# Moving GpSimd's copies, the DMA transposes and ScalarE's joins of k and q within a RetNet and SiLU-MLP kernel

## The chip, the cores and the metric

The kernel runs on one core of a Trainium2 chip. The metric is the device time of one execution in microseconds (us), the median over executions. Spans in traces are some 1.8 us shorter than these times.

## The reference, cut to what matters

```python
# q, k, v: (4, 8, 768, 64) float32; w_in: (512, 2048); w_out: (2048, 512)
for t in range(S):                                  # recurrence, one decay gamma per head
    state = gamma * state + k[:, :, t] (outer) v[:, :, t]
    y[:, :, t] = scale * q[:, :, t] @ state
x = y.transpose(0, 2, 1, 3).reshape(B * S, H * D)   # 3072 x 512
h = x @ w_in
out = (h * sigmoid(h)) @ w_out
```

## The kernel before

The recurrence is done in chunks of 128 steps. A *unit* is one chunk of one batch, 24 in all. Unit m is worked on in *visits*: visit m prepares it, visit m+1 forms its scores, visit m+2 its outputs `y`. Visits stand between *products*: a product is 12 matmuls of 128x512 for one block of the first MLP layer, 2.72 us on TensorE. In the later part there are four products from one visit to the next.

From unit 17 on, k and q are transposed by the DMA, not by TensorE. That takes three steps per tensor: GpSimd parts the float32 words into 16-bit planes, a DMA transposes the planes, ScalarE joins them again. In the code below `n` counts the products, and `far[n]` is the unit whose visit stands behind product n. (TensorE's order is the program's; a list scheduler orders the other engines' queues, within the given limits.)

```python
def fence(done, then):                # one group of y matmuls must wait for another
    i = nc.gpsimd.memset(token, 0.0).ins
    tc.add_manual_dep(i, done.name, sync, reason="fence")
    tc.add_manual_dep(then, i.name, sync, reason="fence")

def part_t(n):                        # GpSimd: q, then k
    ... nc.gpsimd.tensor_copy(out=planes, in_=words)
def turn_t(n):                        # DMA, from the sync queue: q, then k
    ... nc.sync.dma_start_transpose(out=turned, in_=planes)
def join_t(name, n):                  # ScalarE
    ... nc.scalar.copy(out=words, in_=turned)

def product_in(c, f):
    ha, hb = turn(...), turn(...)     # 2 of 3 PSUM banks, in rotation
    ... 8 matmuls into ha, 4 into hb
    hs = hpool.tile(...)              # 3 buffers
    copied[:] = [nc.scalar.activation(out=hs, in_=ha, ...)]      # "evacuation"
    ... behind_copy: the joins
    taken_out[:] = [nc.vector.tensor_tensor(out=hs, in0=hs, in1=hb, op=ALU.subtract)]
    ... behind_next: scaling of k, weight conversion
    nc.scalar.activation(out=hs, in_=hs, func=AF.Silu)

def next_chunk():                     # once in four units: gq, the decay of q, for the next chunk
    for a in range(HP):
        nc.scalar.activation(out=gq[:, a, :], in_=gq[:, a, :], func=AF.Copy, scale=step[:, a:a+1])

for n, (c, f) in enumerate(steps):
    if n - 2 in far:
        behind_copy.append(lambda m=far[n - 2]: join_t("q", m))
        behind_next.append(lambda m=far[n - 2]: scale_k(m))
    if n - 3 in far:
        behind_copy.append(lambda m=far[n - 3]: join_t("k", m))
    product_in(c, f)
    ...
    put_g(1)                          # sync queue: store the product before this one
    behind.get((c, f), lambda: None)()          # the visit, if one stands here
    if n in far:
        turn_t(far[n])
    if n + 1 in far:
        part_t(far[n + 1])
```

## Time and profile before

| | kernel before |
|---|---|
| time, median of 3 runs | 635.18 us (634.76 to 635.78) |
| TensorE busy | 604.1 of 632.9 us |
| TensorE's waits on the fence's memset | 6.0 us |
| GpSimd copies | 14, of 1.03 to 1.91 us |

GpSimd's `token` memsets, one per visit, are marks in time. I call the stretch from the memset of visit 15 (187.72 us in this trace) to that of visit 25 (316.02 us) the *region*: the changed code lies within it, ten stages of 128.30 us together. From the last memset to the end another 316.88 us pass.

The memset distances, in us (stage 16 is the one that ends with the memset of visit 16):

| stage | 16 | 17 | 18 | 19 | 20 | 21 | 22 | 23 | 24 | 25 | sum |
|---|---|---|---|---|---|---|---|---|---|---|---|
| before | 9.95 | 8.73 | 14.43 | 13.87 | 13.87 | 14.15 | 13.84 | 13.51 | 13.19 | 12.76 | 128.30 |

### The profile page before, as it was taken

What the parts mean: (1) busy time and instruction counts of PE and PEld (TensorE: products, weight loads), DVE (VectorE), ACT (ScalarE), POOL (GpSimd) and SP (SyncE); (2) the same over time, 40 slices, a digit from 0 to 9 for tenths busy, and PEclk for the clock granted to TensorE, in tenths of its full rate; (3) what the DMA queues carried; (4) which work ended last, traced back from release to release, by engine and by line L of the source; (5) the groups of instructions that cost most, each with busy time, mean ns of one, the idle gap of its engine ahead of it and who ended that gap; (6) DMA issues with size and microseconds to landing.
All of it is one profiled execution on the core that took longest, in us unless ns stands there. A gap on an engine that the chain in (4) does not pass through costs nothing.

```text
span 632.9 us, 13500 instructions
## 1 busy us (share of the span) xinstructions
PE 604.1 (95%) x5384; PEld 498.5 (79%) x5384; DVE 427.2 (68%) x732; ACT 311.3 (49%) x583; POOL 25.5 (4%) x79
## 2 busy tenths in 40 slices
PE   5788999999999899999999999999999999999997
PEld 3667888887887777778788888888888888888785
DVE  2897997798978868788778674463635544554631
ACT  6657896676565556566568761321312221412311
POOL 3000000000002201121000000000000000000000
PEclk9998999999999999999999999999999999999999
DMA  9996896455678889999757643342433423342301
GB/s 201 212 216 162 233 241 212 160 163 186 221 192 201 219 240 230 235 269 273 248 183 230 189 138 129 111 156 67 165 102 102 166 79 121 134 133 89 111 1 66
DMA packets 137998, 107.31 MB, mean 170 GB/s; under 512 B 94800, under 2 KB 103248, under 8 KB 137936
## 3 DMA queue, kind: packets, MB, share of 16 engines
q1 hardware_dynamic: 135056, 101.21, 56.7%
q10 hardware_dynamic: 2880, 5.24, 2.2%
q8 instruction: 42, 0.69, 0.5%
q14 instruction: 20, 0.16, 0.1%
HBM read 66.06 MB, written 36.70 MB: 162 GB/s over the span
## 4 chain that ended last, share of the span: by engine, by line
PE 86%; DVE 5%; issue 3%; DMA 2%; SPq 1%; ACT 1%; POOL 0%; ACTq 0%; DVEq 0%; POOLq 0%
PE ha L580 25%; PE o L738 20%; PE oa L738 14%; PE hb L580 12%; PE ob L738 7%; PE y L456 4%; PE sc L413 2%; PE sc L423 1%; SPq L149 1%; DMA wf<-in_moe_w_in_dram 1%; DMA kqv<-in_q_dram 1%; PE qp L397 1%; DVE g L588 1%; PE kp L397 1%; DMA wf<-in_moe_w_out_dram 0%
## 5 line engine op out<-in xcount | busy, mean ns | idle before, releaser
L580 PE MATMUL ha<-xt,wi 128*128 128x512 f32 x768 | 193.5, 394 | 0.0
L580 PEld LDWEIGHTS ha<-xt,wi 128*128 128x128 f32 x768 | 143.5, 189 | 31.1 <-DVE g L588 0.5
L738 PE MATMUL o<-wo,gs 128*128 128x512 f32 x576 | 146.3, 389 | 0.0
L738 PEld LDWEIGHTS o<-wo,gs 128*128 128x128 f32 x576 | 108.1, 188 | 22.4
L637 DVE TENSOR_TENSOR gs<-gr,gs 128x512 fp32r<-128x512 f32 x96 | 62.2, 686 | 90.8 <-ACT gs L635 90.8
L635 ACT ACTIVATE gs<-gr 128x512 fp32r<-128x512 f32 x96 | 53.4, 621 | 134.8 <-issue 132.4
L738 PE MATMUL oa<-wo,gs 128*128 128x512 f32 x384 | 118.3, 389 | 0.0
L580 PE MATMUL hb<-xt,wi 128*128 128x512 f32 x384 | 102.9, 390 | 0.5 <-ACT g L584 0.5
L588 DVE TENSOR_TENSOR g<-g,hb 128x512 f32<-128x512 f32 x96 | 65.7, 684 | 40.8 <-ACT g L584 22.7
L580 PEld LDWEIGHTS hb<-xt,wi 128*128 128x128 f32 x384 | 72.0, 188 | 16.0 <-ACT g L584 0.9
L738 PEld LDWEIGHTS oa<-wo,gs 128*128 128x128 f32 x384 | 72.1, 188 | 15.0
L592 ACT ACTIVATE g<-g 128x512 f32<-128x512 f32 x96 | 60.6, 631 | 39.4 <-DVE g L588 39.3
L738 PE MATMUL ob<-wo,gs 128*128 128x512 f32 x192 | 75.2, 392 | 0.4 <-DVE o L747 0.4
L584 ACT ACTIVATE g<-ha 128x512 f32<-128x512 f32 x96 | 56.9, 592 | 32.0 <-PE ha L580 20.9
L638 DVE SCALAR_TENSOR_TENSOR gs<-gs 128x512 fp32r<-128x512 f32 x96 | 62.0, 685 | 0.0
L738 PEld LDWEIGHTS ob<-wo,gs 128*128 128x128 f32 x192 | 36.0, 188 | 9.4 <-DVE o L747 2.1
L197 ACT ACTIVATE ca<-wf 128x512 f32<-128x512 f32 x32 | 21.6, 674 | 15.1 <-DMA wf<-in_moe_w_out_dram 5.6
L456 PE MATMUL y<-qt,state 64*64 64x64 f32 x320 | 17.7, 226 | 7.8 <-POOL token L339 6.0
L456 PE MATMUL y<-qt,mid 64*64 64x64 f32 x384 | 21.8, 227 | 1.6 <-issue 1.6
L208 DVE SCALAR_TENSOR_TENSOR cp<-wf,cp 128x512 f32<-128x512 uint32 x32 | 22.7, 710 | 0.6
L204 DVE SCALAR_TENSOR_TENSOR cs<-ca,cs 128x512 uint32<-128x512 uint32 x32 | 22.1, 691 | 0.9
L746 ACT ACTIVATE o<-o 128x512 f32<-128x512 f32 x10 | 6.0, 600 | 33.4 <-PE o L738 33.0
(84 smaller groups left out, 555.5 us busy)
## 6 DMA issues: line engine op xcount, KB each, us to landing
gd<-g SPq DMA_DIRECT2D x96, 256.0 KB, 3.1
gr<-gd SPq DMA_DIRECT2D x96, 256.0 KB, 2.7
wf<-in_moe_w_out_dram SPq DMA_DIRECT2D x16, 512.0 KB, 4.8
out_dram<-o ACTq DMA_DIRECT2D x20, 256.0 KB, 2.1
wf<-in_moe_w_in_dram SPq DMA_DIRECT2D x16, 256.0 KB, 3.9
wf<-in_moe_w_in_dram SPq DMA_DIRECT2D x32, 128.0 KB, 4.2
kf<-in_k_dram SPq DMA_DIRECT2D x16, 256.0 KB, 4.5
qf<-in_q_dram SPq DMA_DIRECT2D x16, 256.0 KB, 3.9
```

Source lines behind the costliest of these rows:

```text
L197: nc.scalar.activation(out=a.bitcast(FP32), in_=hi.bitcast(FP32), func=AF.Abs, scale=65536.0)
L204: nc.vector.scalar_tensor_tensor(out=s, in0=a, scalar=3, in1=s, op0=ALU.logical_shift_left, op1=ALU.bitwise_or)
L208: nc.vector.scalar_tensor_tensor(out=p.bitcast(FP32), in0=lo, scalar=2.0 ** -52, in1=p.bitcast(FP32), op0=ALU.mult, op1=ALU.mult)
L456: i = nc.tensor.matmul(yp[ts(e, D), o, a, :], lhsT=lhsT, rhs=rhs, start=(e, o) not in started, stop=True, skip_group_check=True).ins
L580: nc.tensor.matmul(hb if i == 2 else ha, lhsT=w_sb[f][:, i, ts(kk, 128)], rhs=xt[c][:, i, kk, :], start=kk == 0 and i != 1, stop=kk == KIN ...
L584: copied[:] = [nc.scalar.activation(out=hs, in_=ha, func=AF.Copy, scale=ONE_E).ins]
L588: taken_out[:] = [nc.vector.tensor_tensor(out=hs, in0=hs, in1=hb, op=ALU.subtract).ins]
L592: nc.scalar.activation(out=hs, in_=hs, func=AF.Silu)
L635: nc.scalar.activation(out=t[:, 0, :], in_=g, func=AF.Copy, scale=HALF)
L637: nc.vector.tensor_tensor(out=t[:, 1, :], in0=g, in1=high, op=ALU.subtract)
L638: nc.vector.scalar_tensor_tensor(out=t[:, 2, :], in0=t[:, 1, :].bitcast(FP32), scalar=-1.0 / EPS, in1=high, op0=ALU.mult, op1=ALU.add)
L738: nc.tensor.matmul(o, lhsT=g, rhs=wo[f][:, i, :], start=first_ and i != 1, stop=last and i != 0)
```

## The change

Its intent: take GpSimd's copies out of the path from the fence's memset to TensorE. A unit's copies now come behind the memset of its own visit, the transposes one product behind the visit, and both joins behind the third product's evacuation.

```diff
@@ fence
         i = nc.gpsimd.memset(token, 0.0).ins
+        fenced[:] = [i]
@@ visit
             finish_y(m - 2, yp)
+
+        if FAR <= m < len(units):
+            with tc.issue_after(fenced[0]):
+                part_t(m)
@@ the loop over products
         if n - 2 in far:
-            behind_copy.append(lambda m=far[n - 2]: join_t("q", m))
             behind_next.append(lambda m=far[n - 2]: scale_k(m))
         if n - 3 in far:
-            behind_copy.append(lambda m=far[n - 3]: join_t("k", m))
+            behind_copy.append(lambda m=far[n - 3]: [join_t(name, m) for name in "qk"])
...
-        if n in far:
-            turn_t(far[n])
-        if n + 1 in far:
-            part_t(far[n + 1])
+        if n - 1 in far:
+            turn_t(far[n - 1])
```

More of the change, by code (lines that the diff above doesn't have):

```diff
@@ L317 @@
     behind_next, behind_copy, half_split = [], [], []
-    taken_out, copied, masked = [], [], []
+    taken_out, copied, masked, fenced = [], [], [], []
     state, steps_of = {}, {}
```

## The prediction

> **What bounds the kernel now.** I read the page first (engine shares and slices), then the waits of TensorE, then GpSimd's timeline, then the chain of waits around a few visits, and last the busy times by stage.
>
> The page's first lines say that TensorE is nearly everything:
>
> ```profile
> span 632.9 us, 13500 instructions
> ...
> PE 604.1 (95%) x5384; PEld 498.5 (79%) x5384; DVE 427.2 (68%) x732; ACT 311.3 (49%) x583; POOL 25.5 (4%) x79
> ```
>
> TensorE is idle for 632.9 - 604.1 = 28.8 us. No change that leaves its matmuls alone, as this one does, can win more than that, and over a third of the 28.8 us lies in the first 55 us, before the changed code begins. What TensorE waited for:
>
> ```profile
> PE y L456 <- issue: 7.7, 7, 1.8
> PE kp L397 <- DMA kqv<-in_k_dram: 7.5, 4, 4.1
> PE y L456 <- POOL token L339: 6.0, 9, 1.1
> ```
>
> (Columns: us in total, times, longest.) The "issue" and k-load rows are all before 54 us. The third row is this change's: a "visit" interleaves the recurrence of one unit (a 128-step chunk of one batch) between the 2.72 us products of the first matmul layer. In it a group of `y` matmuls must wait for another, and the fence between them goes through GpSimd: a one-element memset on `token` that waits for a matmul and releases one. Of its nine waits, seven lie between 194 and 291 us. GpSimd's timeline shows what precedes them (columns: start, duration, engine, line, operation, tiles, count, idle before and its releaser):
>
> ```profile
> 187.72 0.09 POOL L339 MEMSET token<- 1x1 f32 x1 [8.59 <-PE y L456]
> 196.17 1.56 POOL L373 COPY qp<-qf 128x1024 uint16<-128x1024 uint16 x1 [8.36 <-ACT g L592]
> 197.67 0.09 POOL L339 MEMSET token<- 1x1 f32 x1
> ...
> 233.72 1.04 POOL L373 COPY qp<-qf 128x1024 uint16<-128x1024 uint16 x1 [11.82 <-PE sc L413]
> 234.70 0.09 POOL L339 MEMSET token<- 1x1 f32 x1
> 240.19 1.27 POOL L373 COPY kp<-kf 128x1024 uint16<-128x1024 uint16 x1 [5.40 <-DMA kw<-kp]
> ...
> 290.07 0.09 POOL L339 MEMSET token<- 1x1 f32 x1 [3.24 <-PE y L456]
> ```
>
> The q copy of the coming unit cannot start until the `sc<-vf,kf` matmuls of the visit release its buffer; it starts within 0.05 us of that, just ahead of the memset in the queue. Seven memsets in a row (from 197.67 to 276.56 us) have such a copy directly in front; the one at 290.07 has none. TensorE's timeline and the chain of waits show the effect:
>
> ```profile
> 220.97 0.27 PE L456 MATMUL y<-qt,state 64*64 64x64 f32 x1 [1.04 <-POOL token L339]
> ```
>
> ```profile
> 233.67 0.05 issue
> 233.72 0.23 POOL qp L373
> 233.95 0.75 issue
> 234.70 0.10 POOL token L339
> 234.80 0.04 issue
> 234.84 0.46 PE y L456 x16
> ```
>
> The chain leaves TensorE, passes through copy and memset, and returns: this copy, 1% of the work, is on the path that sets the end. The visit at 290 us has no such link in its chain. Busy times by stage (PE, PEld, DVE, ACT, POOL, clock, DMA share, GB/s):
>
> ```profile
> 221.40:235.30 13.90, 13.38 (x181) 11.01 (x177) 9.93 (x17) 8.17 (x12) 1.56 (x3) 1.00 0.79 226
> 277.45:290.70 13.25, 13.25 (x161) 10.97 (x161) 10.90 (x19) 9.02 (x14) 1.61 (x2) 1.00 1.13 279
> ```
>
> The second stage has the same four products and a visit, no copy before its memset, and no TensorE idle time. VectorE works up to 12 of 14 us in the worst stage, ScalarE at most 9.7: neither is the bound.
>
> **What the Trainium skill says.** (1) "PSUM — Partial Sum Buffer", section "Engine vs sequencer instructions": the queues of ScalarE, VectorE and GpSimd are strict FIFO. The trace agrees: at 196.17 us the memset stood behind a copy it has nothing to do with, for 1.5 us. (2) "SBUF — State Buffer", section "Who interferes with whom": a VectorE instruction with two SBUF inputs contends with a GpSimd instruction that reads SBUF, and in a 2-port mode too, under an exclusive lock. The trace agrees in kind: the VectorE scaling of qt beside the copy at 220.87 took 1.52 us against 0.68 us in the visit at 235 with no copy beside it, and the copies themselves take from 1.03 to 1.91 us. (3) "Perfetto Trace Analysis", section "GPSIMD Engine Instruction": GpSimd's spans are unreliable, start-to-start spacing is better. Here both agree: 233.72 to 234.70 is 0.98 us beside a span of 1.04. (4) "DMA: Bandwidth & Descriptors", section "Rules for kernel authors": issue a DMA early and wait late. The change keeps less distance between issue and use, so I check that below; the trace has the landing times.
>
> **The change part by part.** It adds no work and removes none: 7 units, 14 GpSimd copies, 14 DMA transposes, 14 ScalarE joins before and after. Only places move.
>
> Part one, the copies go behind the fence. Before, a unit's copy was called after the product before its visit, and the trace shows the q copies running even one visit earlier. Now both are in the unit's own visit and may issue only after its memset. So all seven TensorE waits should go: 1.11 + 0.81 + 1.04 + 0.52 + 0.80 + 0.50 + 0.78 = 5.56 us of recorded idle time. A second count takes the distance from the first product after one visit to the first after the next, from the chain (198.28, 207.01, 221.43, 235.30, 249.46, 263.32, 277.45, 290.68). The last four-product distance, without a copy, is 13.23 us. The five before it are 14.42, 13.87, 14.16, 13.86 and 14.13, so they lose 1.19 + 0.64 + 0.93 + 0.63 + 0.90 = 4.29 us. The two-product distance ending at 207.01 is 8.73 against 13.23 - 2 x 2.72 = 7.79: 0.94 us. The one ending at 198.28 is 9.95, against 8.68 for the same kind of visit one earlier: 1.27 us. Sum 6.50 us. It exceeds 5.56 us[...], about 0.13 us a visit. I take 6.5 us, since it counts what reaches the next product.
>
> Part two, the transposes go one product behind the visit. Call the memset's time t. In the stage after t = 234.70, the copies end at t + 0.1 + 2 x 1.04 to 2 x 1.56 = t + 2.2 to 3.2; the next product ends about t + 3.3. The transposes occupy the queue for 1.24 us each when they don't wait (median q 1.29), and land 3.3 us (q) and 4.6 us (k) after issue, at most 4.9 and 5.3. So q lands at t + 6.6 to 8.2 and k at t + 9.2 to 9.9.
>
> Part three, both joins behind the third product. A join takes 1.35 us on ScalarE. In this stage the third product's evacuation began at 243.64 and the join of k at 244.12, t + 9.4. Two joins there end at 246.8; the scores that need k (`sc<-qt,kt`) began at 247.55. Even if the third evacuation stays that late (it was late because the join of q stood behind the second product; it should start about 0.7 us earlier now), 0.7 us are left, and k has landed well before its join at t + 10.7. ScalarE's load behind the third product is 0.6 + 2 x 1.35 + 0.63 = 3.9 us against 2.72 us, so the fourth evacuation is over 1 us late. Its bank is wanted again only by the second half of the fifth product, and a visit of 2.3 us lies between. Cost to TensorE: zero.
>
> VectorE's port conflicts move to the mask, qt and state operations after the visit. These are not wanted before the next visit, and VectorE was then idle for 2.00 us waiting for the first product's evacuation, against perhaps 1.5 us of conflicts. Cost: zero.
>
> Sum: 635.2 - 6.5 + 0.2 for a stray late join or fence = 628.9 us, a gain of 1.0%.
>
> **The rivals.** (a) A late join: the k join replaces the fence as TensorE's wait. For it: the pipeline now runs from copy to join inside one visit distance, while DMA share in those stages is already 0.94 to 1.13, and k transposes sat up to 4.25 us in the sync queue. Against it: those long stays were mostly waits on ScalarE's work, and the margin above. If each of seven visits lost 0.5 us, the gain would be 3 us: about 632. (b) VectorE or ScalarE takes over as bound: for it, VectorE at 12 of 14 us in some stages; against it, the 13.25 us stage where TensorE never idles with VectorE at 10.90. If stages stayed near 13.7 us, the time would be 631 to 632. (c) The gain is swallowed later, by a conversion or a store that TensorE then waits for. Against it: from 291 us to the end only 0.7 us of TensorE waits remain in total, and DMA and VectorE load falls after 300 us. If so: 633 to 635. (d) Order on the in-order sync queue gets worse, holding back stores and then ScalarE: 636 or more; the transposes now come when their copies are done, so I think this unlikely.
>
> **Range and chances.** The main case gives 628.5 to 629.3; rivals (a) and (b) in part give up to 632. Predicted 628.9 us, 8 in 10 between 627.8 and 632.0. Faster by over 2% would need 622.5 us, twice what the seven waits hold: 1%. Within 2%: 98.5%. Slower by over 2%: 0.5%.
>
> **What would show it.** Right: the POOL token row of TensorE's waits falls from 6.0 us to under 1 us; each memset stands in GpSimd's timeline ahead of its two copies; stages of four products and a visit take 13.2 to 13.3 us; both joins stand together on ScalarE, ending before `sc<-qt,kt` starts; from 300 us on the trace is the old one, 6.5 us earlier. Wrong: a TensorE wait on kt L387 or qt (rival a); idle TensorE time put down to evacuation or subtraction of `g` (b); new idle time after 300 us (c); stages that stay at 13.9 us although no copy precedes a memset.

## The result, and the profile after

The changed kernel took 633.12 us (632.21 to 633.35, 4 runs) against 635.48 us of the kernel before in the same comparison: ratio 0.996, 95% interval 0.9943 to 0.9977. I had predicted 628.9 us, 627.8 to 632.0. The direction was right, but the gain was less than half of that forecast.

The page of the changed kernel begins:

```profile
span 631.6 us, 13483 instructions
...
PE 606.9 (96%) x5384; PEld 500.1 (79%) x5384; DVE 424.7 (67%) x732; ACT 311.9 (49%) x583; POOL 22.4 (4%) x79
```

TensorE's idle time fell from 28.8 to 631.6 - 606.9 = 24.7 us, while the span fell by only 1.3 us. GpSimd's timeline has the order that was intended in all seven visits; this is one of them:

```profile
233.33 0.09 POOL L339 MEMSET token<- 1x1 f32 x1 [11.06 <-PE y L457]
233.46 1.04 POOL L374 COPY qp<-qf 128x1024 uint16<-128x1024 uint16 x1
234.44 1.05 POOL L374 COPY kp<-kf 128x1024 uint16<-128x1024 uint16 x1
```

And TensorE's waits between 187 and 317 us (total, times, longest) are these, where the kernel before had 5.9 us on the memset:

```profile
PE hb L585 <- ACT g L589: 1.4, 1, 1.4
PE y L457 <- POOL token L339: 0.3, 1, 0.3
PE sc L424 <- ACT kt L388: 0.3, 1, 0.3
```

The memset row keeps 0.3 us, at visit 25, where it was 0.3 us before too. So the fence's waits are gone. The stages show what came in their place:

| stage | 16 | 17 | 18 | 19 | 20 | 21 | 22 | 23 | 24 | 25 | sum |
|---|---|---|---|---|---|---|---|---|---|---|---|
| after | 8.63 | 7.75 | 13.44 | 13.20 | 13.32 | **15.17** | 13.18 | 13.20 | **13.60** | 12.94 | 124.43 |

Six stages have the predicted length to within 0.1 us or so. Stage 21 is 1.02 us *longer* than before, about 1.95 us above 13.2. Stages 18, 24 and 25 hold another 0.8 us. Thus the region fell by 3.87 us, not 6.5.

The traces differ by less still, 1.3 us, for a second reason: the memset of visit 15 stands at 190.31 us, 2.59 us later than in the kernel before, although up to there every engine has the same instructions in the same order in both kernels. That question goes first to the chip.

How did stage 21 get longer? Its chain of waits in the changed kernel (start, duration, what), from the Silu that follows the two joins to the late matmuls:

```profile
246.31 0.62 ACT g L597
246.93 0.49 ACT g L589
...
247.44 0.69 DVE g L593
248.13 0.96 DVE cp L206
...
249.11 0.69 DVE cp L208
...
249.88 0.69 DVE cw L214
250.57 0.60 DVE am L432
251.17 0.33 DVE mid L441
251.50 0.61 DVE qt L365
...
252.44 0.68 ACT gq L312 x2
253.12 0.49 ACT g L589
...
253.66 1.21 PE hb L585 x4
```

ScalarE's timeline in the kernel before, same place:

```profile
244.12 1.35 ACT L387 COPY kt<-kw 128x1024 uint16<-128x1024 uint16 x1
...
245.87 0.58 ACT L584 ACTIVATE g<-ha 128x512 f32<-128x512 f32 x1
...
251.93 0.99 ACT L312 ACTIVATE gq<-gq,step 128x128 f32<-128x128 f32 x3 [1.32 <-DVE qt L364]
252.83 0.57 ACT L584 ACTIVATE g<-ha 128x512 f32<-128x512 f32 x1
```

In both kernels the order is: evacuation of the fourth product; VectorE's subtraction behind it; a weight conversion (`cp`, `cw`) and the mask (`am`) and scaling (`qt`); then the four gq instructions, which overwrite what that scaling reads; and only then the first evacuation after the visit. Before, the fourth evacuation came at 245.87 us, 2.70 us *ahead* of the visit's memset at 248.57. After, two joins stand before it, and it came at 246.83 us, 0.18 us *behind* the memset at 246.65. The whole chain is then late for the second group of matmuls of the second product (`hb`), which needs the bank that the evacuation at 253.03 us frees, and TensorE waits 1.44 us.

The two joins are not all of the lateness. Already the third product's evacuation, which stands in front of them, came 3.71 us ahead of the memset, where it was 4.93 us ahead before; ScalarE had waited for stores of `g` to free its buffers, here and one product earlier:

```profile
240.57 0.60 ACT L589 ACTIVATE g<-ha 128x512 f32<-128x512 f32 x1 [2.20 <-DMA gd<-g]
...
242.94 0.60 ACT L589 ACTIVATE g<-ha 128x512 f32<-128x512 f32 x1 [0.37 <-DMA gd<-g]
```

### The profile page after: what moved, and what is told of

It is laid out like the page before. It is cut to its first block, busy times and chain, and to the rows that moved or that the text cites. A ratio compares the mean times of both kernels' runs of the same rounds, so it can differ in the third digit from the quotient of the medians.

```text
span 631.6 us, 13483 instructions
## 1 busy us (share of the span) xinstructions
PE 606.9 (96%) x5384; PEld 500.1 (79%) x5384; DVE 424.7 (67%) x732; ACT 311.9 (49%) x583; POOL 22.4 (4%) x79
## 4 chain that ended last, share of the span: by engine, by line
PE 82%; DVE 6%; DMA 4%; ACT 3%; issue 2%; SPq 2%; ACTq 0%; DVEq 0%; POOLq 0%
PE ha L585 22%; PE o L740 20%; PE oa L740 14%; PE hb L585 11%; PE ob L740 7%; PE y L457 4%; PE sc L424 2%; DMA wf<-in_moe_w_in_dram 1%; PE sc L414 1%; SPq L149 1%; PE kp L398 1%; DMA kqv<-in_q_dram 1%; DMA gd<-g 1%; PE qp L398 1%; DMA wod<-cw 1%
## 5 line engine op out<-in xcount | busy, mean ns | idle before, releaser
L432 DVE TENSOR_TENSOR am<-sc,decay 128x512 f32<-128x512 f32 x24 | 16.4, 684 | 8.7 <-PE sc L424 8.7
```

## The experiments

The theories. *Two joins plus gq*: two joins in one place make the fourth evacuation late, and in the stage with gq that reaches TensorE. *Late transposes*: the transposes leave the sync queue too late, so the joins wait. *Start-up chance*: the start differs from run to run. I made 12 runs; all gave correct results. I compare regions, because in the three kernels that were traced twice (the two above and e_gq) they repeat to 0.4 us where whole times do not. The other kernels have one trace each.

### Two further looks at the two kernels: r_before, r_after

No edit.

> The kernel before, unchanged, to see how far two looks at one kernel differ. Theory 'start-up chance': the two kernels have the same instructions in the same order on every engine up to the visit at about 188 us, yet the changed kernel's trace was 2.59 us later there (memset on token at 190.31 against 187.72 us); if that is chance, this trace may have that memset anywhere from 186 to 191 us, while the distances between memsets from there on are those of the first trace (9.95, 8.73, 14.4, 13.9, 13.9, 14.2, 13.8, 13.5, 13.2, 12.8) to within 0.4 us. Rival 'the change itself slows the start': the memset is within 0.4 us of 187.72 again. Time 634.5 to 636.5 us either way, ratio 1.000.

> The changed kernel, unchanged. Start-up chance: the memset of the visit that stood at 190.31 us moves by 1 us or more, the later distances stay (8.63, 7.75, 13.44, 13.20, 13.32, 15.17, 13.18, 13.20, 13.60, 12.94), with the 15.17 us stage there again, since its cause lies in the order of instructions. Rival: the memset stays within 0.4 us of 190.31. Ratio 0.996 either way.

r_before: 636.9 us median, ratio 1.0019 (0.999 to 1.0047); memset of visit 15 at 190.09 us; region 128.31 us. r_after: 632.44 us, ratio 0.995 (0.9921 to 0.9979); memset at 191.75 us; region 124.83 us, stage 21 at 15.10 us.

Start-up chance holds. In all 14 profiles that memset lies between 187.72 and 191.75 us, and the very first one, of the kernel before, is the earliest of all. The remainder after the region is 316.7 to 317.7 us in all of them. The region of the kernel before repeats to 0.01 us, that of the changed kernel to 0.4 us, with the same long stage. So in the region the change is worth 3.5 to 3.9 us. The two ratios say 2.5 us (1.5 to 3.6) and 3.2 us (1.3 to 5.0); a single pair of traces could have said anything from nothing to over 7 us.

### The copies behind the fence, alone: e_fence

```diff
 # against the kernel before: only
+        if FAR <= m < len(units):
+            with tc.issue_after(fenced[0]):
+                part_t(m)
-        if n + 1 in far:
-            part_t(far[n + 1])
```

> One part of the change alone: the GpSimd copies behind the fence, but the transposes right behind the visit and the joins where the kernel before has them, q behind the second product and k behind the third. Theory 'two joins in one place': what cost the changed kernel 1.95 us in one stage and 0.4 us in another is that both joins (2 x 1.35 us) stand before the fourth product's evacuation on ScalarE. Then the 15.17 us stage falls to 13.2 to 13.6 us here, and the time is 2 to 2.5 us below the changed kernel's: about 630.8 us, ratio 0.992 to 0.993. Rival 'late transpose': the transposes reach the queue late in any case because stores stand before them; the q join then blocks ScalarE behind the second product, and stages stay at 13.6 us or more, ratio 0.995 to 0.998.

638.24 us, ratio 1.0035 (1.0011 to 1.0058): slower than the kernel before. Region 130.28 us, stages 18 to 24 at 15.27, 13.45, 14.33, 15.96, 13.72, 14.86 and 13.47. The rival was right here, and more strongly than it said. ScalarE's waits in the region, and TensorE's:

```profile
ACT qt L388 <- DMA qw<-qp: 15.5, 7, 2.9
```

```profile
PE hb L585 <- ACT g L589: 5.7, 6, 1.5
```

All seven joins of q wait, 2.2 us on average, and ScalarE's in-order queue hands that to the evacuations and on to TensorE. The fence's waits are gone in this kernel too, but later copies make later transposes, so the join of q must move as well.

Stage 21 shows one thing more. No two joins stand together here, and the fourth evacuation is 1.11 us ahead of the memset of visit 20; still gq starts at 5.36 us behind it and the next evacuation at 6.25 us. VectorE's two `cp` steps took 0.94 and 1.40 us beside the GpSimd copies (in e_joins, without copies there, 0.42 and 0.69 us). So two joins in one place are not the only thing that makes gq late.

### gq behind the evacuation: e_gq and r_gq

```diff
 # against the changed kernel
-            if m > 1 and units[m - 1][1] == 0:
+            if m > 1 and units[m - 1][1] == 0 and m - 1 < 4 * B:
                 next_chunk()
@@ behind part_t(m) in the visit
+        if 4 * B <= m < len(units) and units[m][1] == 0:
+            behind_copy.append(next_chunk)
```

> The changed kernel with one thing moved: the four ScalarE instructions that bring gq to the next chunk stand behind the first evacuation after the visit, not before it (twice in the changed part). Theory 'gq before the evacuation': TensorE's 1.44 us wait at 253.66 us is gone, the 15.17 us stage becomes 13.2 to 13.7 us, and the time falls by 1.5 to 2 us against the changed kernel's (ratio about 0.993 to 0.994). Rival 'two joins' or 'late weight load': VectorE and ScalarE are late there anyhow, and the evacuation would still be late: the stage stays above 14.5 us, ratio 0.996.

> e_gq once more, unchanged, since it is the fastest version so far and its first trace is a single look. If its gain over the changed kernel lies in the gq stage and not in a lucky start, the region is again 122.9 us within 0.4 us with the gq stage at 13.2 to 13.4 us, whatever the start takes, and the ratio to the kernel before is 0.990 to 0.993. If it was luck, the region is 124 us or more.

e_gq: 629.87 us, ratio 0.9898 (0.9877 to 0.992); region 122.92 us; stage 21 at 13.24 us. r_gq, the same kernel again: 631.44 us, ratio 0.9929 (0.9904 to 0.9954); region 122.99 us; stage 21 at 13.20 us. The built order differs from the changed kernel's in nothing but those four ScalarE instructions, in two places. ScalarE in stage 21 (e_gq's memset of visit 20 is at 244.69 us):

```profile
239.67 0.60 ACT L591 ACTIVATE g<-ha 128x512 f32<-128x512 f32 x1
...
243.14 0.58 ACT L591 ACTIVATE g<-ha 128x512 f32<-128x512 f32 x1
...
247.46 0.60 ACT L591 ACTIVATE g<-ha 128x512 f32<-128x512 f32 x1 [0.72 <-ACT xt L504]
248.51 1.28 ACT L312 ACTIVATE gq<-gq,step 128x128 f32<-128x128 f32 x4 [0.45 <-DVE qt L365]
```

The first evacuation after the visit now stands at 2.8 us behind the memset instead of 6.4 us, ahead of gq. The wait on `hb` in this stage is gone. So with gq moved, stage 21 loses its 1.9 us, and the kernel's region is shorter than those of both others. But e_gq does not cut the one link alone: gq was moved after visit 16 too, the transposes of unit 19 left the queue 4 to 5 us behind their memset, not 7.1 us, ScalarE had no wait for a store ahead of the joins, and with the same two joins the fourth evacuation came 1.55 us *ahead* of the memset. The link by itself is tested below, by e_turnact and e_gqturnact.

What is left are stages 23 and 24, at 13.85 and 13.71 us in one trace and 13.90 and 13.73 us in the other, with TensorE waiting 0.35 us on `kt` and 0.4 us on an evacuation. Stage 24 was like this in the changed kernel (13.60 and 13.70 us), but stage 23 was not (13.20 and 13.21 us): a part of the gain is lost again there. The third evacuation before visit 23 waits 2.17 and 2.24 us for a store (1.64 and 1.70 us in the changed kernel).

### Both joins behind the third product, alone: e_joins

```diff
 # against the kernel before: only
-            behind_copy.append(lambda m=far[n - 2]: join_t("q", m))
...
-            behind_copy.append(lambda m=far[n - 3]: join_t("k", m))
+            behind_copy.append(lambda m=far[n - 3]: [join_t(name, m) for name in "qk"])
```

> The kernel before with one part of the change alone: both joins behind the third product; copies and transposes stay where they were. I go by the changed region, from the memset of the visit at 187.72 us to the last one: 128.3 us in both looks at the kernel before, 124.4 and 124.8 us in the changed one. Theory 'two joins make ScalarE late for the fourth product, and gq turns that into a TensorE wait': the seven fence waits stay, the fourth product's evacuation is late, and the stage that holds gq (13.84 and 13.90 us in the kernel before) grows by 0.5 to 1.5 us, the others by 0.2 at most: region 128.8 to 130. Rival 'the joins are free, only later transposes hurt': region 128.3 within 0.3, gq stage 13.9 us. Ratio 1.000 to 1.003.

(The expectation misnames a number: 13.84 and 13.90 us are stage 22 of the kernel before; the gq stage, 21, took 14.15 and 14.13 us.) 639.07 us, ratio 1.0043 (1.0019 to 1.0067); region 130.99 us. Stage 21 grew to 15.53 us, by 1.4 us, by the same chain as in the changed kernel: joins, fourth evacuation, subtraction, conversion, qt, gq, evacuation; here too ScalarE had waited for stores ahead of the joins, 2.31 and 0.68 us. The theory had that stage right, but it missed two things. The scheduler put most q copies behind the memsets of its own accord (I think because the buffers of q are held longer), so only three waits on the fence were left, and this is not a clean test of one part. And stage 23 grew to 16.40 us, where ScalarE waited for stores of `g` to free their buffers (14.0 us of such waits in the region, against 3.2 us in the kernel before).

### gq in the kernel before: e_bgq

The edit of e_gq, made to the kernel before.

> The kernel before with gq's four instructions behind the first evacuation after the visit. Theory 'gq costs only when ScalarE is already late': nothing changes, region 128.3 within 0.4, ratio 1.000. Rival 'gq was a cost in the kernel before too, so e_gq gained something that has nothing to do with the change': region 127 or less, ratio 0.998 or less.

635.83 us, ratio 0.9989 (0.9968 to 1.001); region 127.77 us, 0.5 us less; stages 18, 21 and 23 are 0.3 to 0.5 us shorter (stage 21: 13.85 us against 14.15), stages 20 and 22 0.3 us longer. Between the two expectations, nearer to the first: where ScalarE is not late, the place of gq is worth at most 0.5 us; in the changed kernel 1.5 to 1.9.

### The transposes right behind the visit: e_turn and e_gqturn

```diff
 # against the changed kernel (e_turn) and against e_gq (e_gqturn)
-        if n - 1 in far:
-            turn_t(far[n - 1])
+        if n in far:
+            turn_t(far[n])
```

> The changed kernel with the transposes right behind the visit, not one product later; both joins still behind the third product. Theory 'two joins plus gq': the transposes are issued 2 us or more earlier against the memset, ScalarE's waits on qw go from 1.6 us to about 0, but the gq stage stays above 14.5 us: region 124 to 125. Rival 'late transposes are the cause': gq stage below 14 us, region 123 or less. Third possibility: earlier transposes stand before stores on the sync queue and stall it while the GpSimd copies run; then ScalarE waits more on gd and the region is above 125.

> The changed kernel with both moves: gq behind the evacuation, and the transposes right behind the visit. With gq alone the region took 122.92 us; two stages of 13.85 and 13.71 us were left, with a 0.3 us wait of TensorE on kt and 0.4 us on an evacuation. Theory 'the rest is a join that comes late because the transpose was issued late': both stages fall to 13.2 to 13.4 us, region 122.0 us, the whole 6.5 us that the fence held less nothing; time 629 us, ratio 0.988 to 0.990. Rival: the rest is ScalarE waiting for stores or weights, and the stages stay at 13.7 us, region 122.9.

e_turn: 641.61 us, ratio 1.0071 (1.0042 to 1.01); region 130.94 us, with stage 21 at 16.37 and stage 23 at 16.10 us. e_gqturn: 639.33 us, ratio 1.0038 (1.0015 to 1.0062); region 131.49 us, with 17.00 and 17.46 us. My expectation for e_gqturn, 122.0 us, failed badly; it was the third possibility of e_turn. The joins no longer waited for the transposes, but ScalarE waited for stores. The sync queue in stage 21, in the changed kernel and then in e_turn (start, duration with any wait, instruction):

```profile
252.93 1.83 SPq L603 DMA_DIRECT2D gd<-g  x1
254.85 1.30 SPq L381 DMA_TRANSPOSE qw<-qp  x1
256.27 1.27 SPq L381 DMA_TRANSPOSE kw<-kp  x1
```

```profile
252.99 2.83 SPq L381 DMA_TRANSPOSE qw<-qp  x1
255.91 1.26 SPq L381 DMA_TRANSPOSE kw<-kp  x1
257.29 0.99 SPq L603 DMA_DIRECT2D gd<-g  x2
```

The transposes take the place of a store of `g`, which then issues at 257.29 us and not by 254.76. There are only three buffers for `g`; the next evacuation cannot write until a store has landed.

### The stores off the sync queue: e_turnact, e_gqturnact, e_gqact

```diff
 # against e_turn, e_gqturn and e_gq
-            nc.sync.dma_start(out=g_dram[c, f], in_=g)
+            (nc.scalar if 3 <= c < NC - 1 else nc.sync).dma_start(out=g_dram[c, f], in_=g)
```

> The changed kernel with the transposes right behind the visit, as in e_turn, and the stores of g of the third and fourth chunk taken off the sync queue and issued from ScalarE's queue. Theory 'early transposes hurt because stores stand behind them on the one sync queue, so g's three buffers come free late and ScalarE's evacuation waits': ScalarE's waits on gd fall from 14.2 us to under 4 us, the stage of 16.10 us falls to 13.2 to 13.6, and the region from 130.9 to 124 to 125.5 us, with the gq stage still about 15 us. Rival 'early transposes hurt in themselves, by the load on the DMA engines': region stays above 129 us.

> The same with gq behind the evacuation. Sync queue theory: region 122 to 122.8 us (131.5 without the stores moved), all four-product stages 13.2 to 13.5 us, ratio about 0.988 to 0.990. Rival: ScalarE, which now issues the stores too, becomes late itself: stages of 13.7 us and more, region above 124 us.

> e_gq with the stores of g on ScalarE's queue, transposes where the changed kernel has them. Sync queue theory: with no store before them the transposes are issued at about 3.3 to 4 us after the memset, as I had predicted, not 5.4 to 8.2; the stages of 13.85 and 13.71 us fall to 13.2 to 13.4 and the region from 122.9 to 122.0 us, ratio 0.987 to 0.989. Rival: no change, 122.9 us, or worse by ScalarE's extra work.

| | without: region | with the stores moved: region | time with | ratio with (95%) |
|---|---|---|---|---|
| e_turn, e_turnact | 130.94 | 127.43 | 633.88 | 0.9973 (0.9948 to 0.9998) |
| e_gqturn, e_gqturnact | 131.49 | 125.22 | 632.44 | 0.9949 (0.9927 to 0.9971) |
| e_gq, e_gqact | 122.92 | 127.58 | 633.04 | 0.9964 (0.9931 to 0.9997) |

ScalarE's waits for stores from 187 to 310 us, in e_turn and in e_turnact:

```profile
ACT g L589 <- DMA gd<-g: 14.2, 8, 2.6
```

```profile
ACT g L589 <- DMA gd<-g: 5.8, 2, 3.6
```

Where the transposes stand early, moving the stores away wins 3.5 and 6.3 us back: the damage of e_turn and e_gqturn was in large part the order on the sync queue, not the load on the DMA engines. But none of the three reached what I expected of it (124 to 125.5, 122 to 122.8 and 122.0 us), and e_gqact is 4.7 us worse than e_gq. These are single traces, and not all of typical runs: e_turn's is of its fastest run (637.75 us, the others 641.3 to 642.4), e_gqact's of its slowest (637.06 us, the others 630.7 to 635.7). By median times e_turnact is 7.7 us faster than e_turn, e_gqturnact 6.9 us faster than e_gqturn, and e_gqact 1.6 to 3.2 us slower than e_gq and r_gq. In e_gqact TensorE waits 4.5 us on `kt`, and ScalarE 6.8 us on the transposes of q: with no store ahead of them, the transposes still stand behind weight loads and the conversions' stores, which wait for VectorE (15.4 us and 10.8 us of such waits on the sync queue). My reading of the changed kernel, that a store was what held the transposes back, was only half of it.

e_turnact and e_gqturnact also test the link from gq to TensorE, since they differ by gq alone and the fourth evacuation is equally late in both, 0.11 us ahead of the memset of visit 20 and 0.01 us behind it. The next evacuation stands 5.15 us behind that memset with gq before it, and 3.62 us with gq behind it; TensorE waits 0.39 us for it, and not at all; stage 21 is 13.89 and 13.38 us long.

### What could not be tried

A third buffer for the weight staging or a fourth for `g` would show directly how much these two limits cost; neither fits, as both leave less than the 8 KB per partition that the conversion's buffers need. Why stages 23 and 24 keep 1.1 to 1.2 us in e_gq is traced only as far as the waits named. What makes the start vary by 4 us is open; 3.4 us of it are there by the memset of visit 13 (86.92 to 90.36 us in the 14 traces). It differs between looks at the same kernel, and all the region's findings stand without it.

## Why the prediction was wrong, point by point

**The fence (part one): right in mechanism and size.** The seven waits went, as forecast. I counted 6.50 us by distances rather than 5.56 us by recorded idle time. In e_gq the stages from 16 to 22 have 8.67, 7.79 and five times 13.18 to 13.29 us, the lengths that this count assumed (8.68, 7.79, 13.23). The distance between marks was the better measure of what a wait costs.

**The transposes (part two): a term mis-sized.** I let the sync queue reach them at t + 3.3 us, when the next product ends. In the changed kernel they began between 3.3 and 8.2 us after the memset (5.8, 5.5, 7.1, 8.2, 5.4, 6.7, 3.3), behind stores, loads and conversions in an in-order queue. I knew the issue cost of 1.24 us each and the landing times, which were right (3.1 to 5.0 us to landing, 1.24 to 1.35 us of queue for nearly all), but not the place in the queue. Five of seven joins of q waited for landing, 1.8 us in all.

**The joins (part three): the step that failed.** I wrote that "the fourth evacuation is over 1 us late" and "Cost to TensorE: zero", since its bank is wanted again only much later. The first half was right in direction but too small: it came 0.18 us behind the memset, not 2.70 us ahead. I had put the third evacuation, in front of the joins, 0.7 us earlier than before; it came 1.2 us later against the memset, after waits for stores of 2.20 and 0.37 us. Two joins without such waits leave the fourth evacuation 1.55 us ahead (e_gq). And I followed the evacuation only to its own bank. The same lateness goes through VectorE's subtraction, on to the mask and qt, from there to gq on ScalarE, and so to the *next* evacuation, whose bank TensorE wants at once: it waited 1.44 us. With gq behind that evacuation the wait is gone, and stage 21 falls from 15.17 and 15.10 us to 13.24 and 13.20 us (e_gq, r_gq), though a part of that came earlier in the chain; with the evacuation equally late, moving gq alone takes the wait away too (e_turnact, e_gqturnact). The changed kernel has its own counter-check: at visits 18, 21 and 23, without gq, the fourth evacuation stands 0.02 us behind, 0.22 us ahead and 0.43 us behind the memset, and the next one comes at 2.74, 2.73 and 3.15 us, not at 6.38 us.

**VectorE's conflicts: cost not zero in that stage.** My slack of 2.00 us was read off stage 20. In stage 21 the conversion step `cp` took 0.96 us in the chain beside a GpSimd copy, against 0.35 us in e_joins at the same place without one: 0.6 us of the 1.95 us chain delay. e_fence shows more of it, 1.2 us in two steps. That it would have cost nothing without gq behind it is argued, not shown.

**The rivals.** The loss was mainly (b), ScalarE as the bound of one stage. I had weighed it by the average load of a stage; the average was 9.8 of 15.2 us. What mattered was the order in a queue. Rival (a), a late join, is there with 0.3 to 0.7 us. Rival (d), the order on the sync queue, I thought unlikely. In the changed kernel ScalarE's waits for stores rose from 3.2 to 7.1 us, and two of them made the chain of stage 21 later. The experiments show how much hangs on that order: with the transposes one product earlier the region is 6.1 to 6.5 us longer (one trace). (c) did not occur: the remainder after the region is unchanged.

**The range.** I took the spread of three runs, 1.0 us, for the noise. The start alone varies by 4 us. The region fell 2.4 to 2.8 us short of the forecast (121.8 us, and 0.2 us allowed for a stray wait). From its 3.5 to 3.9 us one expects 631.1 to 632.5 us, against medians of the kernel before of 635.0 to 636.0 us in the comparisons; that is the upper edge of my range or just above it. The medians of the changed kernel, 633.12 and 632.44 us, both lay above the range. What the start adds in the runs without a profile is not known, so I cannot call the rest chance.

## What to carry to other kernels

When an instruction is made late on an in-order engine, follow it through every queue that waits for it until the bound engine is reached; freeing its own buffer in time is not enough, and the average load of an engine did not show it here. Parts of a pipeline may pay only together: here the copies alone and the joins alone lost 2.0 and 2.7 us of the region, and copies and joins with the transposes left early 2.6, while all three together gained 3.5 to 3.9. To measure changes of under 1%, time a stretch between two fixed marks in the trace, and take the noise from several traces of the same kernel.

## What the Trainium skill lacked or had wrong

- "DMA: Bandwidth & Descriptors", section "Issuing engines are not separate DMA queues", says that issuing from several engines only saves issue time, which is usually small beside the DMA. Here the order on the issuing queue counted for more: a transpose held the sync queue 1.24 to 1.35 us against 0.32 to 0.43 us of a plain DMA that did not wait; issuing transposes one product earlier lengthened the region to 130.94 us from 124.43 and 124.83; and taking only the stores off that queue changed it from 131.49 to 125.22 us in one kernel and from 122.92 to 127.58 us in another (one trace each, the last of a slow run; by medians 639.33 to 632.44 us, and 629.87 to 633.04 us).
- I found no page with the issue time of a DMA transpose for this chip by name ("DMA: Bandwidth & Descriptors" has cycle counts only for unnamed earlier generations, in its part on trn3 B0); the runs give 1.24 us at least.
- I found no page on how much the start of a kernel varies: the same instructions took from 187.72 to 191.75 us up to the memset of visit 15 in 14 traces.
